# A table of half slots for the first two batches, replaced row by row, in an attention and ELU-MLP kernel

## The chip, the core and the metric

One core of one Trainium2 chip runs the whole program. The metric is the device time of one execution in microseconds (us); the figure that counts is the median of several runs. A profiled execution of the kernel before gives the trace from which all rows below are read. The engines are PE (TensorE: matmuls, with PEld for its weight loads), DVE (VectorE), ACT (ScalarE), POOL (GpSimd) and SP (SyncE, which here only issues DMAs). Each engine works through its own list of instructions in a fixed order; engines wait for each other by semaphores.

## The reference

Eight batches of twelve heads, 448 positions, head size 64. Queries and keys are normalised (RMS norm with a gain), scores are softmaxed and multiplied with the values; the result, one row of 768 per position, goes through a two-layer MLP with ELU.

```python
q_n, k_n = (rmsnorm(q, g_q), rmsnorm(k, g_k))
scores = scale * np.matmul(q_n, k_n.transpose(0, 1, 3, 2))
attn = np.exp(scores - np.max(scores, axis=-1, keepdims=True))
attn = attn / (np.sum(attn, axis=-1, keepdims=True) + 1e-09)
attn_out = np.matmul(attn, v)
h = x @ w_in                       # x: 3584 x 768, w_in: 768 x 2048
g = np.where(h > 0.0, h, np.exp(np.minimum(h, 0.0)) - 1.0)
out = g @ w_out                    # w_out: 2048 x 768
```

## The kernel before

**Tiles.** Heads are taken in pairs, 48 pairs `p`, six to a batch. The 896 query rows of a pair make seven tiles of 128, so there are 336 tiles `T` (pair `T // 7`), 42 to a batch. Each operand is split into a high and a low float16 part, and products are summed from several matmuls.

**Steps of a pair.** `load_qk` (L330) brings q and k of the pair in (448 KB, tile `nat`). `qk_square` (ACT, L353), `qk_sum` (DVE), `qk_root` (ACT, L361 and L362), `qk_newton` (DVE) and `qk_norm` (POOL) normalise; `k_high`, `q_high` (ACT, L391 and L401), `k_low`, `q_low` make the float16 parts; `qk_transpose` (SP, L420, two DMA transposes, one of q and one of k) turns them into `qkt`; `q_swap` (SP, L427, two copies of 112 KB inside the chip's memory) adds the halves in swapped order, and every score tile needs all three.

**Steps of a tile.** `s_mm` (PE, L537) makes the scores in one of the PSUM banks `s0` to `s4`; `s_max` (DVE, L544), `s_exp` (ACT, L558), `s_z`, `s_rec`. In batch 0 (T below 42) the probabilities are turned on PE: `s_diag` (POOL, L574) makes a diagonal matrix, `s_pe` (PE, L582) multiplies with it, `s_hi` (ACT, L592) copies the result out of the bank, which is then free. From T = 42 on, `s_hi` (L598) and `s_lo` (DVE, L603) write float16 parts, and `s_tr` (SP, L613) is a DMA transpose into `ptall`. `attend` (PE, L630) multiplies with v once per pair; `x_high` (ACT, L637) and `x_low` hand the result to the MLP.

**Weights.** Sixteen pieces of `w_in` and 24 of `w_out` are brought in by `conv.load` (SP, L229; 768 KB and 512 KB) and split in steps: `s_act` (L237) and `s_bits` (L240) on ACT, `s_shift` (L245), `s_join` (L269), `s_scale` and `s_low` (L290) on DVE, `s_high` on POOL, and `s_sums` (L142, column sums on PE). All of it happens while batches 0 and 1 go through attention.

**MLP.** `mlp(b)` makes 576 matmuls for batch b, first the layer of `w_in` (L730), then that of `w_out` (L741). For batch 0 it can begin in earnest only when all six pairs of batch 0 have been attended to. Afterwards these matmuls fill PE between the score tiles of the next batch.

**What sets the order.** A half slot `h` is a place in a list, not a time: for h from -18 up, the program writes down all steps due at h - 0.5 and at h, loads first, then other steps, then the matmuls of h, then the late PE steps. So h fixes the order of the instructions on each engine and nothing else; an engine that is behind simply works the list off later. The half slots stand in the table `SCHED` (from L864): `qk` (one row a pair, in the order of the steps above, from `load_qk` to `q_swap`), `v`, `scan` (loads of v, for its scale), `wi` and `wo` (one row a weight piece), `tile` (one row a tile), `mm` (half slot of each `s_mm`), `att`, `rate` (MLP matmuls due by each h), `m`, `m1`, `m2`. Rows are given for the first two batches; the last row of `qk`, `v`, `scan` and `tile` is repeated for all later pairs, batches and tiles with a fixed distance.

```python
for p in range(NP):
    k = p if p < 12 else 11
    put([h + HP * (p - k) for h in SCHED["qk"][k]], [
        (load_qk, p), (qk_square, p), (qk_sum, p), (qk_root, p), (qk_newton, p), (qk_norm, p),
...
    run_tasks(h - 0.5, 1)
    run_tasks(h - 0.5, 2)
    run_tasks(h, 0)
    run_tasks(h, 1)
```

All DMAs are issued by SP in this order, on one queue.

Of the kernel before, what the change touches and what calls it, by code (L numbers as in the profile page):

```python
# [1137 lines left out]
```

## Time and profile before

| what | value |
|---|---|
| median of 3 runs | 1234.65 us (1234.53 to 1234.99) |
| the profiled execution's own time | 1238.01 us |
| its span from first to last instruction | 1236.2 us |
| PE busy | 1185.0 us (96%) |
| DVE busy | 863.4 us (70%) |
| ACT busy | 808.2 us (65%) |
| POOL busy | 499.1 us (40%) |
| DMA moved | 181.29 MB |

The shares are means over stages that differ: in the first of 40 slices PE is busy for 3 tenths and from the tenth slice on for 9 tenths or more, while DVE and ACT stand at 8 or 9 tenths in the first nine slices and at 5 to 7 tenths later. So the table is to be read by stage.

### The profile page before, as it was taken

What the parts mean: (1) busy time and instruction counts of PE and PEld (TensorE: products, weight loads), DVE (VectorE), ACT (ScalarE), POOL (GpSimd) and SP (SyncE); (2) the same over time, 40 slices, a digit from 0 to 9 for tenths busy, and PEclk for the clock granted to TensorE, in tenths of its full rate; (3) what the DMA queues carried; (4) which work ended last, traced back from release to release, by engine and by line L of the source; (5) the groups of instructions that cost most, each with busy time, mean ns of one, the idle gap of its engine ahead of it and who ended that gap; (6) DMA issues with size and microseconds to landing.
All of it is one profiled execution on the core that took longest, in us unless ns stands there. A gap on an engine that the chain in (4) does not pass through costs nothing.

```text
span 1236.2 us, 21611 instructions
## 1 busy us (share of the span) xinstructions
PE 1185.0 (96%) x7180; PEld 736.4 (60%) x7180; DVE 863.4 (70%) x2042; ACT 808.2 (65%) x1705; POOL 499.1 (40%) x789
## 2 busy tenths in 40 slices
PE   3778899999999999999999999999999999999998
PEld 2556455765557655675557655675557655675576
DVE  7889999888885588666885588566785588542410
ACT  7889999867775477556675477556675477542310
POOL 4767554644444343444344343444344344320000
PEclk9889999999999999999999999999999999999999
DMA  8766889879667876687668867687568766551000
GB/s 302 224 155 189 190 185 188 164 175 193 134 137 165 177 137 135 138 195 153 128 131 162 184 139 131 137 199 150 130 131 165 181 137 134 109 108 31 1 16 30
DMA packets 403024, 181.29 MB, mean 147 GB/s; under 512 B 368352, under 2 KB 385376, under 8 KB 402912
## 3 DMA queue, kind: packets, MB, share of 16 engines
q1 hardware_dynamic: 402912, 179.91, 66.8%
q8 instruction: 57, 0.93, 0.3%
q14 instruction: 55, 0.45, 0.1%
HBM read 68.35 MB, written 11.01 MB: 64 GB/s over the span
## 4 chain that ended last, share of the span: by engine, by line
PE 82%; DVE 4%; issue 0%; ACT 0%; POOL 0%; ACTq 0%
PE m L741 23%; PE m L730 22%; PE s L741 12%; PE s L730 11%; PE s L537 9%; PE av L630 7%; DVE p L603 1%; DVE st L544 0%; DVE gall L687 0%; DVE w32s L269 0%; DVE e L674 0%; DVE wlos L312 0%; PE av L142 0%; DVE wts L245 0%; ACT s L558 0%
## 5 line engine op out<-in xcount | busy, mean ns | idle before, releaser
L544 DVE TENSOR_REDUCE st<-s 128x1 f32<-128x448 f32 x336 | 207.3, 620 | 168.4 <-PE s L537 166.8
L741 PE MATMUL m<-gall,whos 128*128 128x448 f16 x1024 | 282.0, 353 | 0.0
L562 POOL TENSOR_SCALAR st<-st 128x1 f32<-128x1 f32 x294 | 74.3, 253 | 482.2 <-ACT s L558 475.2
L741 PEld LDWEIGHTS <-whos 128*128 128x128 f16 x1536 | 221.7, 144 | 73.4 <-issue 0.7
L730 PE MATMUL m<-x,whi 128*128 128x448 f16 x926 | 256.4, 353 | 0.3 <-DVE e L674 0.3
L558 ACT ACTIVATE s<-s,st 128x448 f32<-128x448 f32 x294 | 178.1, 606 | 100.0 <-DVE st L544 98.6
L730 PEld LDWEIGHTS <-whi 128*128 128x128 f16 x1536 | 149.8, 98 | 137.2 <-issue 1.7
L598 ACT ACTIVATE p<-s,st 128x448 f16<-128x448 f32 x294 | 185.1, 631 | 61.2 <-DMA ptall<-p 35.9
L603 DVE SCALAR_TENSOR_TENSOR p<-s,st,p 128x448 f16<-128x448 f32 x294 | 198.6, 677 | 30.8 <-ACT p L598 29.6
L537 PE MATMUL s<-qkt 128*128 128x448 f16 (+1 forms) x768 | 184.8, 360 | 18.0 <-ACT gall L592 5.3
L741 PE MATMUL m<-gall,wlos 128*128 128x448 f16 x512 | 181.3, 354 | 0.0
L730 PE MATMUL m<-x,wli 128*128 128x448 f16 x463 | 163.3, 353 | 0.0
L741 PE MATMUL s<-gall,whos 128*128 128x448 f16 x512 | 140.8, 353 | 0.0
L741 PEld LDWEIGHTS <-wlos 128*128 128x128 f16 x768 | 110.6, 144 | 41.6 <-issue 6.8
L730 PE MATMUL s<-x,whi 128*128 128x448 f16 x450 | 124.0, 352 | 0.0
L730 PEld LDWEIGHTS <-wli 128*128 128x128 f16 x768 | 75.1, 98 | 74.2 <-issue 6.8
L537 PEld LDWEIGHTS <-qkt 128*128 128x128 f16 (+1 forms) x768 | 63.3, 101 | 79.4 <-issue 34.5
L684 ACT ACTIVATE gall<-e,ui 128x448 f16<-128x448 f32 x128 | 85.1, 665 | 32.1 <-DVE e L679 32.1
L630 PE MATMUL av<-ptall,vt 128*64 128x448 f16 x924 | 94.7, 353 | 0.6 <-DVE most L145 0.6
L687 DVE SCALAR_TENSOR_TENSOR gall<-e,ui,gall 128x448 f16<-128x448 f32 x128 | 88.0, 688 | 8.5 <-ACT gall L684 8.3
L382 POOL TENSOR_TENSOR nat<-nat,r 128x896 f32<-128x896 f32 (+1 forms) x48 | 84.4, 1758 | 21.8 <-DVE r L372 13.5
L741 PE MATMUL s<-gall,wlos 128*128 128x448 f16 x256 | 90.6, 354 | 0.0
(120 smaller groups left out, 1696.5 us busy)
## 6 DMA issues: line engine op xcount, KB each, us to landing
nat<-in_qk SPq DMA_DIRECT2D x48, 448.0 KB, 4.6
...
qkt<-qkt SPq DMA_DIRECT2D x96, 112.0 KB, 4.1
...
whos<-in_w_in SPq DMA_DIRECT2D x10, 768.0 KB, 6.6
ptall<-p SPq DMA_TRANSPOSE x336, 3.0
```

Source lines behind the costliest of these rows:

```text
L382: nc.gpsimd.tensor_tensor(out=n[:, a:], in0=n[:, a:], in1=r[:, a:], op=ALU.mult)
L537: nc.tensor.matmul(ps[r0 : r0 + n, :S], lhs, qq[:, 1, h * S : h * S + S], start=(t == 0), stop=(t == 2),)
L544: nc.vector.tensor_reduce(out=st[:, 0:1], in_=pss[T][:, :S], axis=AX.X, op=ALU.max, negate=True)
L558: nc.scalar.activation(e, ps, AF.Exp, bias=st[:, 0:1], accum_out=st[:, 1:2])
L562: (nc.vector if by_pe(T) else nc.gpsimd).tensor_scalar(out=st[:, 1:2], in0=st[:, 1:2], scalar1=1e-9, scalar2=2.0 ** (UP - 7) if by_pe(T) e ...
L598: nc.scalar.activation(p16[:, :S], pss[T][:, :S], AF.Copy, scale=stats[T][:, 2:3])
L603: nc.vector.scalar_tensor_tensor(out=p16[:, S:], in0=ps[:, :S], scalar=r, in1=p16[:, :S], op0=ALU.mult, op1=ALU.subtract)
L630: nc.tensor.matmul(av[64 * h : 64 * h + 64, :S], vs[:, h], ps[h], start=(k == 0), stop=(k == len(terms) - 1),)
L684: nc.scalar.activation(g[:, 0], e, AF.Copy, scale=ui)
L687: nc.vector.scalar_tensor_tensor(out=g[:, 1], in0=e, scalar=ui, in1=g[:, 0], op0=ALU.mult, op1=ALU.subtract)
L730: nc.tensor.matmul(ph[:, :S], w[:, c, :], x[:, r, :], start=(c == 0 and i == 0), stop=last)
L741: nc.tensor.matmul(py[:, :S], w, g[:, r, :], start=(f == 0 and i == 0), stop=last)
```

## The change

The table `SCHED` is replaced; no function, tile or transfer changes, and every step is still there once. Nearly every row of `qk`, `v`, `scan`, `wi`, `wo`, `tile`, `rate`, `m1`, `m2`, `mm` moves some entries by a half to several half slots. Two rows of each kind:

```diff
     "qk": [
-        [-18, -17, -16.5, -14.5, -13.5, -13.5, -10, -10.5, -10, -4.5, -9.5, -6.5, -3.5, -3.5],
-        [-16.5, -15.5, -10, -10, -9.5, -2.5, -1.5, -1, 1, 3, 2.5, 4, 6.5, 11.5],
...
-        [5, 8.5, 12.5, 13, 19, 19.5, 20.5, 22, 22, 34.5, 31, 32.5, 35, 35],
...
+        [-16, -16, -15.5, -15, -13, -12.5, -10, -9.5, -9.5, -8, -9, -7.5, -5, -4.5],
+        [-18, -14, -13, -8, -7.5, -4.5, -3, -3, 1, 3, 3.5, 6.5, 4.5, 11.5],
...
+        [5.5, 8.5, 11, 15.5, 15.5, 19.5, 21.5, 20, 23.5, 33.5, 28.5, 32, 35, 37.5],
...
     "tile": [
...
-        [0, 1, 2, 3, 4, 4.5, 6, 9, 5],
...
+        [0, 1, 2, 3.5, 4.5, 5, 6, 13.5, 7.5],
...
     "mm": [
-        [-1, -2, 1, -1, 5, 8, 7, 12, 16, 15, 20, 20, 21, 24, 23, 30, 29, 31, 34, 34, 38, 37, 42,
...
+        [-1, -4, 0, 1, 6, 7, 8, 12, 16, 17, 19, 20, 21, 24, 24, 29, 28, 30, 32, 36, 39, 40, 40,
```

What this does to the order of instructions is shown at three places.

**SP at the start of the program, before.** `nat_143` is pair 0, `nat_159` pair 1, `nat_239` pair 2, `qkt_216` pair 0; `in_w_in` is a weight piece, `in_v` a piece of v.

```order
L330 DMA nat_143<-in_qk 128x896
L190 DMA ggt_145<-in_gg 128x128
L330 DMA nat_159<-in_qk 128x896
L229 DMA raws_133<-in_w_in 128x1536
L172 DMA gall_131<-in_v 128x512 x2
L229 DMA raws_133<-in_w_in 128x1536
L229 DMA whos_121<-in_w_in 128x1536 x2
L420 DMA_TRANSPOSE qkt_216<-t16_194 128x7x128 x2
L427 DMA qkt_216<-qkt_216 64x896 x2
L330 DMA nat_239<-in_qk 128x896
```

The same place now, where `nat_143` is pair 1, `nat_156` pair 0, `nat_241` pair 2 and `qkt_210` pair 0:

```order
L330 DMA nat_143<-in_qk 128x896
L190 DMA ggt_145<-in_gg 128x128
L330 DMA nat_156<-in_qk 128x896
L229 DMA raws_133<-in_w_in 128x1536 x2
L172 DMA gall_131<-in_v 128x512
L229 DMA whos_121<-in_w_in 128x1536 x2
L420 DMA_TRANSPOSE qkt_210<-t16_198 128x7x128
L172 DMA gall_131<-in_v 128x512
L330 DMA nat_241<-in_qk 128x896
L420 DMA_TRANSPOSE qkt_210<-t16_198 128x7x128
L427 DMA qkt_210<-qkt_210 64x896 x2
```

Pair 0, the one that is needed first, is now loaded third instead of first, and a piece of v and pair 2 are loaded between the two transposes of pair 0, ahead of its swap.

**ACT around tiles 20 and 21, before.** `x1` is the output of pair 1; `ex_891` is `s_exp` of tile 20 (bank `s0`), `ex_923` that of tile 21 (bank `s1`, the first tile of pair 3); `raws` are weight steps, `t16` and `qkt` steps of pairs 4 and 5.

```order
L637 ACTIVATE x1_124<-av_72,vs_474 128x448
L558 ACTIVATE ex_880,st_846<-s4_71,st_846 128x448
L391 ACTIVATE t16_883<-nat_602 128x7x64
L237 ACTIVATE wts_134<-raws_133 128x768
L558 ACTIVATE ex_891,st_876<-s0_67,st_876 128x448
L592 ACTIVATE ptall_132<-s2_69 112x4x128
L353 ACTIVATE qkt_898<-nat_835 128x896
L240 ACTIVATE raws_133<-raws_133 128x768
L592 ACTIVATE ptall_132<-s3_70 112x4x128
L401 ACTIVATE t16_883<-nat_602 128x7x64
L558 ACTIVATE ex_923,st_908<-s1_68,st_908 128x448
```

The same place now, where `ex_913` is tile 20 and `ex_929` tile 21:

```order
L637 ACTIVATE x1_124<-av_72,vs_455 128x448
L558 ACTIVATE ex_850,st_837<-s4_71,st_837 128x448
L592 ACTIVATE ptall_132<-s0_67 112x4x128
L237 ACTIVATE wts_134<-raws_133 128x768
L391 ACTIVATE t16_870<-nat_599 128x7x64
L240 ACTIVATE raws_133<-raws_133 128x768
L592 ACTIVATE ptall_132<-s2_69 112x4x128
L353 ACTIVATE qkt_885<-nat_829 128x896
L401 ACTIVATE t16_870<-nat_599 128x7x64
L558 ACTIVATE ex_913,st_893<-s0_67,st_893 128x448
L558 ACTIVATE ex_929,st_911<-s1_68,st_911 128x448
```

Four steps that came after the exponential of tile 20 (the `s_hi` of bank `s2`, the square of pair 5, `s_bits`, `q_high` of pair 4) now stand ahead of it.

**PE at the same place, before.** The two matmuls of tile 21 into `s1` read `qkt_661` (pair 3); those of tile 20 into `s0` read `qkt_390` (pair 2).

```order
L582 MATMUL s1_68<-dgz_824,ex_771 112x128 x4
L582 MATMUL s0_67<-dgz_830,ex_738 112x128 x4
L537 LDWEIGHTS qkt_661
L537 MATMUL s1_68<-qkt_661 128x448
L537 LDWEIGHTS qkt_661
L537 MATMUL s1_68<-qkt_661 128x448
L537 LDWEIGHTS qkt_390
L537 MATMUL s0_67<-qkt_390 128x448
```

The same place now, with `qkt_385` for pair 2 and `qkt_670` for pair 3:

```order
L582 MATMUL s0_67<-dgz_806,ex_777 112x128 x4
L537 LDWEIGHTS qkt_385
L537 MATMUL s0_67<-qkt_385 128x448
L537 LDWEIGHTS qkt_385
L537 MATMUL s0_67<-qkt_385 128x448
L730 LDWEIGHTS wli0_105
L730 MATMUL m0_73<-x0_123,wli0_105 128x448
L582 MATMUL s2_69<-dgz_863,ex_839 112x128 x4
L537 LDWEIGHTS qkt_670
L537 MATMUL s1_68<-qkt_670 128x448
```

Tile 20 now comes before tile 21, with one MLP matmul and one `s_pe` between them.

## Rows read from the trace of the kernel before

**Rows 1.** Busy time by stage (header names the columns).
```profile
core 0: us, PE busy (x) PEld busy (x) DVE busy (x) ACT busy (x) POOL busy (x), PEclk, DMA share, GB/s
0.00:20.00 20.00, 2.15 (x27) 1.59 (x27) 13.21 (x35) 13.86 (x17) 5.95 (x10) 1.00 0.81 267
20.00:146.00 126.00, 99.80 (x814) 69.46 (x815) 113.03 (x307) 116.84 (x221) 86.34 (x95) 0.95 0.70 205
146.00:220.00 74.00, 70.65 (x488) 38.09 (x485) 71.86 (x170) 71.99 (x141) 37.75 (x55) 1.00 0.87 178
220.00:1160.00 940.00, 939.82 (x5475) 576.62 (x5474) 653.94 (x1514) 593.41 (x1310) 367.95 (x627) 1.00 0.70 144
```

**Rows 2.** Timeline of ACT, 70 to 86 us: start, us; idle before it in brackets.
```profile
75.83 0.94 ACT L237 ACTIVATE wts<-raws 128x768 f32<-128x768 f32 x1
80.67 0.63 ACT L558 ACTIVATE ex<-s,st 128x448 f32<-128x448 f32 x1 [3.91 <-PE s L582]
...
81.30 0.59 ACT L592 ACTIVATE ptall<-s 112x512 f32<-112x512 f32 x1
81.78 0.95 ACT L353 ACTIVATE qkt<-nat 128x896 f32<-128x896 f32 x1
82.62 1.92 ACT L240 ACTIVATE raws<-raws 128x768 uint16<-128x768 uint16 x1
84.28 0.69 ACT L592 ACTIVATE ptall<-s 112x512 f32<-112x512 f32 x1
84.86 0.56 ACT L401 ACTIVATE t<-nat 128x448 f16<-128x448 f32 x1
85.32 0.63 ACT L558 ACTIVATE ex<-s,st 128x448 f32<-128x448 f32 x1
```

**Rows 3.** Timeline of PE, 70.5 to 81 us.
```profile
74.35 0.35 PE L537 MATMUL s<-qkt 128*128 128x448 f16 x1 [1.34 <-DMA qkt<-t]
76.82 1.28 PE L537 MATMUL s<-qkt 128*128 128x448 f16 x3 [2.12 <-DMA qkt<-qkt]
```

**Rows 4.** Issues on SP, 60 to 80 us: start, us to issue.
```profile
67.39 0.58 SPq L229 DMA_DIRECT2D raws<-in_w_in  x1
68.70 1.23 SPq L420 DMA_TRANSPOSE qkt<-t  x1
70.03 1.18 SPq L427 DMA_DIRECT2D qkt<-qkt  x2
```

**Rows 5.** DMA issues at 67.4 and 70.6 us: KB, us from issue to landing.
```profile
raws<-in_w_in SPq DMA_DIRECT2D x1, 768.0 KB, 5.8
...
qkt<-qkt SPq DMA_DIRECT2D x1, 112.0 KB, 6.1
```

**Rows 6.** Timeline of ACT, 0 to 32 us: the first squares and the first exponential.
```profile
4.32 0.95 ACT L353 ACTIVATE ptall<-nat 128x896 f32<-128x896 f32 x1 [2.30 <-DMA nat<-in_qk]
7.55 0.95 ACT L353 ACTIVATE ptall<-nat 128x896 f32<-128x896 f32 x1 [2.29 <-DMA nat<-in_qk]
...
22.74 0.63 ACT L558 ACTIVATE ex<-s,st 128x448 f32<-128x448 f32 x1 [0.27 <-DVE st L544]
```

**Rows 7.** Timeline of PE, 0 to 45 us: the first score tile's second matmul.
```profile
20.53 2.77 PE L537 MATMUL s<-qkt 128*128 128x448 f16 x7 [1.36 <-DMA qkt<-qkt]
```

**Rows 8.** Timeline of ACT, 30 to 50 us: its waits.
```profile
33.62 0.95 ACT L353 ACTIVATE qkt<-nat 128x896 f32<-128x896 f32 x1 [0.63 <-PE s L537]
...
42.16 0.60 ACT L592 ACTIVATE ptall<-s 112x512 f32<-112x512 f32 x1 [2.32 <-PE s L582]
```

**Rows 9.** Two later pairs: SP and PE around the attention; all `ptall` landings, 460 to 1060 us.
```profile
559.56 1.25 SPq L613 DMA_TRANSPOSE ptall<-p  x1
...
566.64 2.25 PE L630 MATMUL av<-ptall,vt 128*64 128x448 f16 x22
...
589.89 2.25 PE L630 MATMUL av<-ptall,vt 128*64 128x448 f16 x22
...
DMA to landing us min/median/max: 2.5/3.0/5.5
```

More of the change, by code (lines that the diff above doesn't have):

```diff
@@ L1043 @@
-        [0, 1, 2, 3, 4, 4.5, 6, 9, 5],
+        [-0.5, 1, 2.5, 4, 5, 5, 7],
+        [-2, -0.5, 0, 1, 1.5, 4, 4.5],
+        [2, 3, 4, 4, 5, 10, 10.5],
+        [1.5, 5, 6.5, 9.5, 9.5, 11, 13],
+        [9.5, 10.5, 10.5, 11, 12.5, 12.5, 14],
+        [9, 10, 10, 11, 14.5, 17, 18],
+        [10, 13, 13, 13, 16, 16.5, 17.5],
+        [13.5, 14, 15.5, 15.5, 18, 18.5, 19],
+        [17, 19.5, 20.5, 21.5, 21.5, 22, 24],
+        [18.5, 19, 20, 20, 20, 20.5, 24],
+        [21, 22, 22.5, 23.5, 24.5, 25, 28],
@@ new lines @@
+        [20.5, 21.5, 21.5, 23, 25.5, 26, 27.5],
+        [22.5, 24.5, 26, 26, 26.5, 27, 29.5],
+        [24.5, 27, 27.5, 28, 29, 29.5, 31],
+        [25.5, 28, 29, 29.5, 29.5, 30.5, 34],
+        [31, 33, 33.5, 35, 35, 36.5, 37.5],
+        [29, 32.5, 33, 34, 34, 35, 36.5],
+        [32, 36.5, 37.5, 37.5, 38, 39, 39.5],
+        [33.5, 36, 37.5, 40, 40.5, 41.5, 42.5],
+        [36.5, 37.5, 38.5, 38.5, 40, 41.5, 42.5],
+        [40.5, 41, 42, 43, 44, 46, 46.5],
+        [41, 42, 42, 42, 44, 45.5, 47],
@@ new lines @@
+        [43, 44, 45, 45.5, 46, 47, 48.5],
+        [45, 46, 46.5, 46.5, 47, 48, 49.5],
+        [48, 50, 50, 51, 51.5, 52.5, 53.5],
+        [48.5, 48.5, 49, 51, 52.5, 53.5, 56],
+        [50, 50.5, 54, 55.5, 56, 56, 57],
+        [51.5, 56, 57, 57, 58, 58.5, 59.5],
+        [56, 57, 57.5, 57.5, 59, 59.5, 62],
+        [56, 59, 59.5, 60.5, 61, 61, 62.5],
+        [59, 60, 62, 63, 64, 65, 67.5],
+        [60, 60, 64.5, 66, 67.5, 67.5, 68.5],
+        [61.5, 63.5, 64.5, 65, 66, 69.5, 70.5],
+        [64.5, 66.5, 67, 68, 70.5, 70.5, 73],
@@ new lines @@
+        [67.5, 68.5, 69.5, 70.5, 71, 71, 73],
+        [69.5, 70.5, 71, 72, 72, 73, 75.5],
+        [73, 74.5, 75, 76, 77.5, 77.5, 80],
+        [73, 73.5, 73.5, 74.5, 74.5, 77, 77.5],
+        [75.5, 76, 78, 79, 80, 81, 82],
+        [76.5, 82, 82.5, 82.5, 84, 84, 84.5],
+        [78, 79.5, 79.5, 80.5, 80.5, 83, 86],
+        [81.5, 82.5, 83.5, 84, 85.5, 86.5, 87],
+        [82.5, 83.5, 86.5, 87.5, 88.5, 91, 93],
+        [84, 86, 86, 89.5, 90, 91.5, 95],
+        [87.5, 88, 88, 91.5, 93, 94, 99],
@@ new lines @@
+        [91, 92, 94, 94, 94, 95, 96.5],
+        [90.5, 92.5, 95, 95, 96, 98, 100],
+        [94, 95, 97, 97, 98, 100, 102],
+        [96.5, 97.5, 98.5, 99.5, 100.5, 100.5, 101],
+        [101, 101.5, 101.5, 102.5, 103.5, 105, 109],
+        [96.5, 103, 103.5, 104, 104, 105.5, 107.5],
+        [102.5, 103, 103, 105, 107, 108, 111],
+        [105.5, 107, 108.5, 109, 110, 110, 110.5],
+        [107.5, 109, 111, 111.5, 113, 113, 116],
+        [109.5, 110.5, 112, 112.5, 113, 113, 113],
+        [112, 112.5, 112.5, 113, 114, 114, 115.5],
@@ new lines @@
+        [113, 115, 115, 115, 116.5, 117.5, 124.5],
+        [115, 116, 116, 117, 117.5, 118.5, 120.5],
+        [116.5, 116.5, 118.5, 118.5, 119.5, 120, 123],
+        [119.5, 121, 121, 122, 123.5, 126, 128.5],
+        [120, 121.5, 122, 122.5, 123.5, 124.5, 127],
+        [122, 124, 126.5, 127, 127.5, 128.5, 130],
+        [125, 126, 126, 126.5, 127.5, 127.5, 130],
+        [128.5, 128.5, 129, 129.5, 131.5, 132, 141],
+        [127.5, 130, 130, 131, 131.5, 132.5, 134.5],
+        [130, 131.5, 132, 132, 132.5, 133.5, 135],
@@ new lines @@
+        [132, 133.5, 133.5, 134.5, 135.5, 137, 138],
+        [135.5, 137.5, 138.5, 140, 141.5, 142, 142],
+        [134.5, 136, 138.5, 138.5, 142, 142, 144],
+        [135, 135, 138.5, 141, 141.5, 141.5, 142],
+        [140.5, 140.5, 143.5, 144, 145, 146, 150],
+        [142.5, 143, 143, 143.5, 144, 144, 148],
+        [146.5, 147, 147, 148.5, 148.5, 149, 149],
+        [148.5, 148.5, 152.5, 154, 154, 154.5, 156.5],
+        [148, 149.5, 150, 151.5, 151.5, 152, 155],
+        [147.5, 148.5, 151.5, 154, 155, 155, 157],
@@ new lines @@
+        [152, 152.5, 153, 154, 155.5, 155.5, 157.5],
+        [156.5, 157.5, 157.5, 157.5, 159, 159.5, 162.5],
+        [158.5, 158.5, 159.5, 160.5, 161.5, 162.5, 162.5],
+        [157.5, 158.5, 160, 160, 161, 162.5, 165],
+        [158.5, 159.5, 162, 162.5, 165, 166.5, 168.5],
+        [163, 163.5, 163.5, 163.5, 163.5, 166, 168],
+        [163.5, 163.5, 165, 166, 167, 167, 169],
+        [165, 167, 167.5, 168.5, 169.5, 169.5, 169.5],
+        [169.5, 170, 171, 171.5, 173, 174, 176],
+        [168, 168.5, 171.5, 171.5, 175, 175.5, 179],
@@ L1070 @@
-        [2.5, 3.5, 3.5, 5.5, 6.5],
-        [1.5, 2.5, 3, 3.5, 4.5],
+        [0.5, 1, 2.5, 6.5, 11.5],
+        [1.5, 3, 3.5, 6, 6],
+        [2.5, 5.5, 6, 8, 9],
+        [2, 3.5, 3.5, 6, 7.5],
+        [2, 2, 3.5, 4.5, 8],
+        [0.5, 1, 2, 3, 5],
+        [1.5, 2.5, 4, 5, 12.5],
+        [1, 2.5, 3, 5, 6],
+        [2.5, 4.5, 5, 6, 6.5],
+        [1.5, 3.5, 4.5, 6, 6.5],
+        [1.5, 2, 3.5, 4.5, 10],
+        [1, 1, 2.5, 5.5, 6.5],
+        [1, 1.5, 2, 5, 8],
+        [2, 2, 3.5, 7.5, 9.5],
@@ L1074 @@
     "m2": [
[L1075 to L1080 removed]
+        [5, 7.5, 8],
+        [4.5, 12, 16],
+        [2.5, 10.5, 13],
+        [8.5, 10, 14.5],
+        [3.5, 7.5, 13],
+        [4.5, 7, 9.5],
         [1, 2, 3],
```

156 lines of the change are left out of this document (26 added, 130 removed), and 127 rows, old and new, of the table SCHED.

## The prediction

> **What bounds the kernel now.** I read the stages first [rows 1]. From 220 us on, PE is busy for 939.82 of 940 us: nothing that happens on the other engines there can be seen in the time, and the number of matmuls does not change. From 146 to 220 us PE is busy for 70.65 of 74 us, so at most 3.35 us are to be had. From 0 to 146 us PE has 101.95 us of work in 146 us. That is where the time can move. The MLP of batch 0 cannot begin before the last pair of batch 0 has been attended to, and until then PE lives on what the others hand it. Of those, ACT is the fullest: 116.84 of 126 us from 20 to 146 us, against 113.03 on DVE and 86.34 on POOL. So up to 146 us the pace is ACT's list, and a microsecond comes off the end only if ACT's idle time shrinks there or if its list becomes shorter.
>
> ACT's idle time, 9.16 us in that stage, lies for the most part in three places, which its timeline shows. At 80.67 us ACT had sat idle for 3.91 us in front of an exponential [rows 2]; at 42.16 us for 2.32 us in front of an `s_hi`, and at 33.62 us for 0.63 us [rows 8]. PE shows why for the first: its list is in order, and at 74.35 and 76.82 us it stood, for 1.34 and 2.12 us, in front of the first tile of pair 3 until a transpose and then a swap of that pair had landed [rows 3], while tile 20, which ACT wanted, was ready behind it. And SP shows why the swap was late: a weight piece of 768 KB was issued at 67.39 us, ahead of the transpose at 68.70 and the swaps at 70.03 [rows 4]. It took 5.8 us to land, and a swap of only 112 KB took 6.1 us [rows 5]. Transfers land one behind the other, and a small one pays for the large one ahead of it.
>
> **Part 1: tile 20 goes ahead of tile 21.** On PE the tile that needs the swap of pair 3 now comes after tile 20 and an `s_pe`, and on ACT four steps come ahead of the exponential of tile 20 that used to follow it. Counted from start to start of the next row, these are 0.48 us (`s_hi`, 81.30 to 81.78), 0.84 us (square, to 82.62), 1.66 us (`s_bits`, to 84.28) and 0.46 us (`q_high`, 84.86 to 85.32) [rows 2], together 3.44 us. So even if PE served tile 20 as late as now, ACT would idle for only 3.91 - 3.44 = 0.47 us; if PE serves it earlier, the whole 3.91 us go. The swap itself is not sooner: the same weight piece still stands ahead of the second transpose of pair 3, and now the load of pair 5 stands ahead of the swap too. What is late next is therefore the exponential of tile 21, which follows directly; it stood at 85.32 us, 8.6 us after the last swap landed (70.6 + 6.1 = 76.7), so there is room. I take -3.7 us (-3.9 to 0).
>
> **Part 2: the start.** Pair 0 is loaded third. The two loads of equal size were followed by squares at 4.32 and 7.55 us, each of which had waited for its load [rows 6], so the first data that anything can be done with come 3.23 us later. In front of the first exponential (22.74 us) ACT has the same steps in both lists. Lower bound: ACT idled for 2.29 us ahead of 7.55 us anyway, and only the first square, 0.95 us, is pushed behind it: +1.0 us. Upper bound: the whole 3.23 us, and on top a wait for the two loads that now go between the transposes of pair 0. The first tile already waited 1.36 us for its swap at 20.53 us [rows 7], and a load of half the size of a weight piece ahead of a swap costs about half of what separates 6.1 us from the 2.5 us that a transfer takes at the least [rows 5, 9], so up to +1.8 us, together +5.0 us. I take +3.0 us, close to the 3.23 us that are a row: ACT's list gives less, but the scores need the late pair.
>
> The Trainium skill, "DMA: Bandwidth & Descriptors", Specifications, gives 435 GB/s as the ceiling of the fabric. By it, 448 KB and the 64 KB of gains ahead would delay pair 0 by about 1.2 us, an estimate, and with 1.2 in place of 3.0 us the sum below would come to -4.7 us; the rows say 3.23 us, and I go by them.
>
> **Part 3: what the late start absorbs.** The `s_hi` at 42.16 us waited on PE, which stood in front of pair 1's first tile until its swap had landed. Around that swap SP's list is the same: transpose, load of pair 3, transpose, one weight piece, swap. If those transfers land when they do now, an ACT that is 3 us later finds them done, and the 0.63 and 2.32 us of waiting [rows 8] are eaten: -3.0 us. If the transposes, whose input comes from ACT and POOL, are as late as everything else, nothing is eaten: 0. I take -2.9 us, since ACT's list reaches this tile more than twenty steps after the first exponential, whereas pair 1's float16 parts come early in it. Against this, the new order brings two tight places behind the first exponentials: the square of pair 2 is followed by its `qk_root` with one exponential in between, so the sum on DVE has only 0.63 us of cover, and the fifth weight piece's `s_act` comes ahead of that square. I put these at +0.7 us (0 to 2).
>
> **Part 4: the rest.** Up to the last `s_hi` of batch 0, ACT has one `s_bits` less and one exponential more ahead of it; an `s_bits` takes up to 1.92 us and an exponential 0.63 us with its read of the sum behind it [rows 2]. For a smaller `w_out` piece the difference is smaller; I take 0 (-1.1 to 0). From 146 to 220 us all engines stay full in both orders, and I see no reason for a change either way: 0 (-1.5 to +1.5).
>
> From batch 2 on, the repeated rows move too. The transpose of the last tile of each pair goes from 5 to 7.5 half slots after its tile. Today the last transpose ahead of an attention is issued at 559.56 us and the attention begins at 566.64 us, 7.08 us later; a landing takes 3.0 us in the median [rows 9], so 4.08 us are spare. A half slot does not hold SP up, though: between the old and the new place its list has nothing that waits for PE, so the issue stays where its data let it be. 0 us.
>
> **Sum.** -3.7 + 3.0 - 2.9 + 0.7 + 0 + 0 = -2.9 us. The profiled execution would go from a span of 1236.2 us to 1233.3 us and from 1238.01 us to 1235.1 us; the median stood 3.36 us below the profiled execution, so 1234.65 - 2.9 = 1231.75, say 1231.8 us.
>
> **The rivals.**
>
> *The delay is rigid (slower).* Everything in front of pair 1 hangs on pair 0: its transposes, too, slide by 3 us, so the waits at 33.62 and 42.16 us stay, and the swap of pair 3, now behind one more load, stalls the exponential of tile 21 by as much as that of tile 20 today. Then +3.0 + 0.7 with nothing gained: 1234.65 + 3.7 = 1238.4 us. For it: the in-order queue of transfers. Against it: the 3.44 us of ACT work that now covers tile 20 do not depend on pair 3. It decides if tile 21's exponential begins after about 88 us.
>
> *The late load costs little.* If ACT's list alone sets the start (+1.0 instead of +3.0 us), the sum is -4.9 us: 1229.8 us. If ACT's waits in part 3 vanish as well and PE's 3.35 us from 146 to 220 us shrink by half, it is 1228 us. The ceiling that the Trainium skill states ("DMA: Bandwidth & Descriptors", Specifications) would point this way.
>
> *One wait is exchanged for another.* The stall of tile 20 goes, but the new order loses as much between 86 and 146 us, where ACT hardly waits now (9.16 us idle in the whole stage, of which 3.91, 2.32 and 0.63 us are the waits above [rows 2, 8]): about 1234.6 us. The change would then not do what it says.
>
> *Every later pair pays.* Should the later transposes of part 4 really be issued 2.5 half slots later, the 4.08 us of slack would be used up, since one pair takes 589.89 - 566.64 = 23.25 us for 14 half slots [rows 9], so 2.5 of them are 4.15 us. Every tenth of a microsecond beyond it costs 36 pairs 3.6 us. At 0.25 us a pair: 1244 us. Nothing in SP's list speaks for it.
>
> **How the numbers follow.** About 0.2%, 2.5 us, is what a measurement of this kernel can tell from no change, so faster means below 1232.2 us and slower above 1237.1 us. My forecast (1230 to 1233.5 us) has 0.45, rather less than two thirds of it on the faster side; the cheap start 0.20, all faster; the exchange 0.15, all same; the rigid delay 0.16, mostly slower; the later pairs 0.04, slower. Faster 0.28 + 0.20 = 0.48; same 0.17 + 0.15 = 0.32; slower 0.20. Leaving out the best part of the cheap start and the later pairs, the range is 1227.0 to 1238.5 us.
>
> **What would show it right or wrong.** In the profile after: the first square at about 7.5 us and the first exponential at 25 to 26 us (part 2); the wait in front of an `s_hi` near 42 us gone (part 3); the wait near 80 us below 0.5 us and no DMA named by PE there (part 1); the last attention of batch 0 some 3 us earlier than now; PE without idle time from 220 us on (part 4). A first exponential at 23.5 us would show the cheap start, a stall in front of the first tile of pair 3 or a last attention of batch 0 that comes no earlier than now, the rigid delay.

## The result and the profile after

The changed kernel is **slower**: 1244.1 us in the median (1242.55 to 1245.0) against 1234.78 us; the ratio, as estimated from the runs, is 1.0067 (the two medians alone give 1.0075), with a 95% interval of 1.0054 to 1.0081, so 6.7 to 10 us. The forecast was 1231.8 us and a range that ended at 1238.5 us. The profiled execution took 1245.0 us, with a span of 1243.2 us.

Busy time by stage of the kernel after (same columns as [rows 1]):

```profile
0.00:20.00 20.00, 0.85 (x13) 0.84 (x14) 11.18 (x31) 12.43 (x15) 4.35 (x10) 1.00 0.70 241
20.00:146.00 126.00, 98.05 (x807) 68.68 (x808) 111.43 (x298) 115.29 (x216) 81.29 (x92) 0.93 0.71 203
146.00:220.00 74.00, 67.84 (x468) 35.52 (x465) 69.58 (x167) 71.85 (x141) 39.70 (x56) 1.00 0.89 182
220.00:1160.00 940.00, 939.22 (x5479) 576.78 (x5477) 664.78 (x1524) 599.02 (x1313) 380.24 (x629) 1.00 0.70 145
```

Beside [rows 1], PE is idle for 1.3 us more in the first stage (20 - 0.85 against 20 - 2.15), 1.75 us more in the second, 2.8 us more in the third and 0.6 us more in the last. So the loss lies ahead of 220 us, two fifths of it (2.8 of the 7.0 us between the spans of the two profiled executions) from 146 to 220 us, where I had put a zero.

ACT's timeline after, at the start and in front of tiles 20 and 21 (to be read against [rows 6] and [rows 2]):

```profile
7.58 0.95 ACT L353 ACTIVATE ptall<-nat 128x896 f32<-128x896 f32 x1 [5.56 <-DMA nat<-in_qk]
...
14.21 0.62 ACT L391 ACTIVATE t<-nat 128x448 f16<-128x448 f32 x1
...
25.88 0.63 ACT L558 ACTIVATE ex<-s,st 128x448 f32<-128x448 f32 x1 [0.59 <-DVE st L544]
...
85.61 0.62 ACT L558 ACTIVATE ex<-s,st 128x448 f32<-128x448 f32 x1
...
86.36 0.63 ACT L558 ACTIVATE ex<-s,st 128x448 f32<-128x448 f32 x1
```

Several of my signs are there: the first square at 7.58 us, the first exponential 3.1 us late, and the exponentials of tiles 20 and 21 without a wait. And still tile 20's comes 4.9 us later than in the trace of before, and the last attention of batch 0, which I had put 3 us earlier, comes later: its `x_high` begins at 149.59 us, against 145.16 us. New waits stand ahead of tile 20, which the trace of before does not have:

```profile
45.55 0.63 ACT L558 ACTIVATE ex<-s,st 128x448 f32<-128x448 f32 x1 [0.93 <-DVE st L544]
53.14 0.63 ACT L558 ACTIVATE ex<-s,st 128x448 f32<-128x448 f32 x1 [0.71 <-DVE st L544]
...
68.48 0.60 ACT L592 ACTIVATE gall<-s 112x512 f32<-112x512 f32 x1 [1.60 <-PE s L582]
```

### The profile page after: what moved, and what is told of

It is laid out like the page before. It is cut to its first block, busy times and chain, and to the rows that moved or that the text cites. A ratio compares the mean times of both kernels' runs of the same rounds, so it can differ in the third digit from the quotient of the medians.

```text
span 1243.2 us, 21624 instructions
## 1 busy us (share of the span) xinstructions
PE 1185.5 (95%) x7180; PEld 736.0 (59%) x7180; DVE 871.9 (70%) x2042; ACT 813.2 (65%) x1705; POOL 506.6 (41%) x789
## 4 chain that ended last, share of the span: by engine, by line
PE 79%; DVE 2%; ACT 2%; issue 0%; DMA 0%; ACTq 0%
PE m L741 22%; PE m L730 21%; PE s L741 11%; PE s L730 10%; PE s L537 8%; PE av L630 7%; DVE p L603 0%; DVE st L544 0%; DVE wlos L312 0%; ACT raws L240 0%; ACT p L598 0%; DMA raws<-in_w_out 0%; ACT s L558 0%; DVE w32s L269 0%; DVE e L674 0%
## 5 line engine op out<-in xcount | busy, mean ns | idle before, releaser
L544 DVE TENSOR_REDUCE st<-s 128x1 f32<-128x448 f32 x336 | 205.4, 615 | 124.7 <-PE s L537 123.9
L562 POOL TENSOR_SCALAR st<-st 128x1 f32<-128x1 f32 x294 | 86.4, 294 | 464.1 <-ACT s L558 451.9
L687 DVE SCALAR_TENSOR_TENSOR gall<-e,ui,gall 128x448 f16<-128x448 f32 x128 | 94.7, 741 | 9.1 <-ACT gall L684 9.1
L382 POOL TENSOR_TENSOR nat<-nat,r 128x896 f32<-128x896 f32 (+1 forms) x48 | 81.5, 1698 | 31.2 <-DVE r L372 25.1
```

Of the source, the lines that this page charges most:

```text
L382: nc.gpsimd.tensor_tensor(out=n[:, a:], in0=n[:, a:], in1=r[:, a:], op=ALU.mult)
L544: nc.vector.tensor_reduce(out=st[:, 0:1], in_=pss[T][:, :S], axis=AX.X, op=ALU.max, negate=True)
L562: (nc.vector if by_pe(T) else nc.gpsimd).tensor_scalar(out=st[:, 1:2], in0=st[:, 1:2], scalar1=1e-9, scalar2=2.0 ** (UP - 7) if by_pe(T) e ...
L687: nc.vector.scalar_tensor_tensor(out=g[:, 1], in0=e, scalar=ui, in1=g[:, 0], op0=ALU.mult, op1=ALU.subtract)
```

## Experiments

Times are given as ratios to the kernel before on the same chip, with 95% intervals; 0.0010 is 1.2 us. Before itself spread from 1232.5 to 1241.0 us over these comparisons.

### Another execution of the kernel before

Run `again` is the kernel before, unchanged.

> The kernel before, unchanged, profiled once more. Its profiled execution stood 3.36 us above its median. If that excess lay in the waits for the swaps of pairs 1 and 3, as two runs with the same order up to 130 us suggest (1.0 to 1.4 us and 2.6 to 2.8 us there, against 2.32 and 3.91 us), an execution near 1235 us shows about 1.2 us near 41 us and 2.7 us near 77.5 us, and its attention of pair 5 begins some 2 us earlier than at 141.8 us. If the excess lies elsewhere, those two waits are 2.3 and 3.9 us again.

It took 1235.24 us with a span of 1233.4 us, 2.8 us less than the execution that I had read. Its waits near 42 and 80 us on ACT:

```profile
42.30 0.60 ACT L592 ACTIVATE ptall<-s 112x512 f32<-112x512 f32 x1 [2.37 <-PE s L582]
...
77.18 0.63 ACT L558 ACTIVATE ex<-s,st 128x448 f32<-128x448 f32 x1 [1.25 <-PE s L582]
```

The first is as long as in [rows 8], the second is 1.25 us where [rows 2] show 3.91 us. So half of the expectation falls, and the other half is stronger than expected. Two runs further down, `last_rows` and then `late_new`, have the order of before up to this place and beyond it, and are thus two more executions of it here:

```profile
41.26 0.60 ACT L592 ACTIVATE ptall<-s 112x512 f32<-112x512 f32 x1 [1.04 <-PE s L582]
...
77.51 0.64 ACT L558 ACTIVATE ex<-s,st 128x448 f32<-128x448 f32 x1 [2.57 <-PE s L582]
```

```profile
41.09 0.60 ACT L592 ACTIVATE ptall<-s 112x512 f32<-112x512 f32 x1 [1.36 <-PE s L582]
...
77.52 0.64 ACT L558 ACTIVATE ex<-s,st 128x448 f32<-128x448 f32 x1 [2.77 <-PE s L582]
```

In these three executions the two waits differ one by one, but together they make 3.6, 3.6 and 4.1 us, and the exponential of tile 20 begins at 77.2 to 77.5 us. In the execution read ahead of the prediction they make 6.2 us, and it begins at 80.67 us.

Why the second wait differs, PE's timeline and the granted clock show. First the execution read ahead of the prediction (stage rows, then PE):

```profile
70.00:76.00 6.00, 3.36 (x34) 2.27 (x30) 4.14 (x10) 6.00 (x11) 4.68 (x5) 1.00 1.08 249
76.00:82.00 6.00, 5.18 (x30) 3.96 (x31) 3.79 (x10) 2.09 (x5) 1.91 (x3) 0.51 0.20 74
```

```profile
78.61 2.03 PE L582 MATMUL s<-dgz,ex 128*112 128x128 f32 x8
```

Then the other execution of the same kernel:

```profile
76.00:82.00 6.00, 4.18 (x37) 3.24 (x34) 6.00 (x12) 4.82 (x8) 3.62 (x4) 1.00 0.01 4
```

```profile
75.08 0.73 PE L537 MATMUL s<-qkt 128*128 128x448 f16 x3 [2.10 <-DMA qkt<-qkt]
...
76.04 1.10 PE L582 MATMUL s<-dgz,ex 128*112 128x128 f32 x8
```

In both, PE stood for more than 2 us in front of the swap of pair 3. In the first, which had stood 1.34 us in front of the transpose before that [rows 3], the granted clock then fell to half (0.51, the lower of its two levels, 1.2 and 2.4 GHz), and the eight matmuls for which the exponential waited took 2.03 us; in the second, where the stop in front of the transpose was 0.44 us, it stayed full and they took 1.10 us. Of the 2.66 us by which the two waits differ, 0.90 us are the longer stop in front of the transpose, and the rest lies behind the swap, where PE was slower. The 3.91 us were thus a transfer that was late and an engine at half speed, and the second part is not in every execution: in `last_rows` and `late_new` the granted clock from 76 to 82 us was 0.86 and 0.74.

### What makes the start late

`start_new` and `start_old` mix the two tables by the mean of the old and the new half slot (`OTHER` is the other table; `start_new` starts from the kernel before, `start_old` from the changed one):

```diff
+def take(old, new, f):
+    return [n if f((o + n) / 2) else o for o, n in zip(old, new, strict=True)]
...
+part(lambda h: h < 24)
```

> The table of before with the entries of the changed table wherever the mean of old and new half slot lies below 24 (up to about 45 us); everything behind is as before. It asks whether a late start is carried through or absorbed. Theory A, a delay of the start is rigid: the start costs what the trace after shows up to tile 20, some 4.5 us, and most of it comes out at the end: 1237 to 1240 us, and the first exponential at 25 to 26 us. Theory B, the delay is absorbed by the waits of ACT near 42 and 80 us, and what was lost was lost behind: 1234 to 1236 us.

> The counterpart: the changed table with the entries of before wherever the mean half slot lies below 24. Theory A, rigid start: the 4.5 us come back, 1238.5 to 1241 us, and about as much as the loss between 86 and 224 us (4 to 6 us) less the gain at tile 20 (3.9 us) remains. Theory B, the loss is all behind the start: 1243 to 1244 us. If start and rest simply add, the differences of this run and of the run with the new start alone add up to that of the whole change.

`start_new`: 1.0061 (1.0047 to 1.0075). `start_old`: 1.0045 (1.0031 to 1.0058); in it the shift of one weight piece stands ahead of the `s_act` whose result it should shift, so its columns of the hidden layer are garbage, and the amount of work is the same. Neither theory holds: both halves lose. Nor do they simply add: 0.0061 and 0.0045 make 0.0106, more than the whole change. The traces say the same. `x_high` of pair 5, the last of batch 0, begins at 141.69 us in `again` and at 149.59 us in the kernel after, 7.9 us later; in `start_new` and then in `start_old` it is 5.2 and 5.0 us late:

```profile
146.88 0.62 ACT L637 ACTIVATE x<-av,vs 128x448 f16<-128x448 f32 x1
```

```profile
146.67 0.63 ACT L637 ACTIVATE x<-av,vs 128x448 f16<-128x448 f32 x1
```

What the new start costs in the changed kernel is the difference between that kernel and `start_old`: 2.9 us at this place, and 1.0067 - 1.0045 = 0.0022, 2.7 us, in the time. (Of the repeated rows, `start_new` took over only that of the tiles.)

`loads_old`, `start_loads`, `start_pieces` and `start_between` take the start apart. The first is the changed kernel with one edit, the others are the kernel before with one edit each:

```diff
+SCHED["qk"][0][0], SCHED["qk"][1][0] = -18, -16
```
```diff
+SCHED["qk"][0][:3], SCHED["qk"][1][0] = [-16, -16, -15.5], -18
```
```diff
+SCHED["wi"][:2] = [
+    [-15, -14, -12, -13, -8.5, -12.5, -7, -4.5, -2.5],
+    [-15, -12.5, -9.5, -7, -7, -7, -6, 0.5, 7.5],
+]
```
```diff
+SCHED["qk"][2][0], SCHED["scan"][0][1] = -5, -6
```

> The changed table with nothing but the first loads of pair 0 and pair 1 put back in the old order (half slots -18 and -16). If the 3.1 us by which the first exponential came later are due to the order of these two loads alone and are carried to the end: first exponential back at 22 to 23 us and 1240.5 to 1241.5 us. If the rest of the new start makes up for it or loses it anyway (a transpose and a swap behind a load of pair 2): 1243 to 1244 us.

> The kernel before with only the first loads exchanged: pair 1 first, pair 0 third, the square of pair 0 where its data let it be. The prediction counted 3.0 us for this (3.23 us of lateness carried through): first exponential at 25.7 us. The rival 'the late load costs little': k_high of pair 0 stands behind the first weight piece's s_act and s_bits on ACT anyway (12.01 us), so it moves by 1 us or less and the first exponential stays below 24 us; time 1235 to 1236 us.

> The kernel before with only the rows of the first two weight pieces from the changed table: the second piece is loaded earlier, and ACT reads it ahead of the first k_high. In the run loads_old the first exponential stayed 3.3 us late although pair 0 was loaded first again, and ACT stood in front of these pieces until they had landed (9.69 and 11.60 us). If that is what makes the start late: k_high of pair 0 at about 14 us in place of 12.0, the first exponential 2 us later, and 1236 to 1238 us. If the loads between the transposes of pair 0 make the start late: first exponential at 22.7 us as before and no change.

> The kernel before with only two loads moved: the load of pair 2 and one piece of v go between the two transposes of pair 0, ahead of its swap. If these make the start late: the second transpose lands 2 to 4 us later (18.6 us before), and the first exponential comes at 24.5 to 26 us. If the transposes get through all the same: first exponential near 22.7 us. Time in both cases 1234.5 to 1237 us, since the waits near 42 us and 77 us take up a part.

`loads_old`: 1.0065 (1.0051 to 1.0080), nothing gained. Its ACT timeline:

```profile
9.69 0.89 ACT L237 ACTIVATE wts<-raws 128x768 f32<-128x768 f32 x1 [0.91 <-DMA raws<-in_w_in]
11.60 0.90 ACT L237 ACTIVATE wts<-raws 128x768 f32<-128x768 f32 x1 [1.02 <-DMA raws<-in_w_in]
...
14.04 0.62 ACT L391 ACTIVATE t<-nat 128x448 f16<-128x448 f32 x1
```

Pair 0 is there early, but ACT now stands in front of two weight pieces that come ahead of `k_high` (L391), and that step begins at 14.04 us, against 14.21 us in the kernel after. The load order, on which my 3.0 us rested, is hidden behind the pieces. By itself it costs little: in `start_loads` the first exponential begins at 23.72 us, 0.98 us later than in [rows 6], and the time is 1.0003 (0.9994 to 1.0013). `start_pieces` alone does more (1.0010, 0.9999 to 1.0020):

```profile
11.21 0.92 ACT L237 ACTIVATE wts<-raws 128x768 f32<-128x768 f32 x1 [1.01 <-DMA raws<-in_w_in]
...
13.66 0.62 ACT L391 ACTIVATE t<-nat 128x448 f16<-128x448 f32 x1
...
25.40 0.63 ACT L558 ACTIVATE ex<-s,st 128x448 f32<-128x448 f32 x1
...
49.06 0.66 ACT L558 ACTIVATE ex<-s,st 128x448 f32<-128x448 f32 x1
```

The first exponential is 2.66 us late; the last line is that of tile 8. In `start_between` (1.0004, 0.9994 to 1.0015) it begins at 24.11 us, 1.37 us late, and ACT waits 2.37 us for a transpose:

```profile
21.05 0.58 ACT L391 ACTIVATE t<-nat 128x448 f16<-128x448 f32 x1 [2.37 <-DMA qkt<-t]
...
24.11 0.63 ACT L558 ACTIVATE ex<-s,st 128x448 f32<-128x448 f32 x1
```

So three edits, one by one, delay the start by 1.0, 2.7 and 1.4 us, and the changed kernel, which has them all, by 3.1 us: the longest one covers most of the others, and undoing one that is covered (`loads_old`) gives nothing. No run undoes the pieces alone.

### Pair 1: is it the order of its transposes?

The rows of SP's order around the swap of pair 1 read alike in both kernels, but in the changed one k is transposed ahead of q. The swap copies q, and SP waits for it:

```profile
SPq L427 <- DMA qkt<-t: 2.9, 1, 2.9
```

(SP's waits of the kernel after, 25 to 45 us: total, times, longest; in another execution of before that row reads 0.5 us.) `after_q_first` puts q first again in the changed kernel, `before_k_first` puts k first in the kernel before, and `after_repaired` adds to the former the old loads, the old first two weight pieces and one step on DVE:

```diff
+SCHED["qk"][1][9:13] = [3.5, 3, 4.5, 6.5]
```
```diff
+SCHED["qk"][1][9:13] = [2.5, 3, 6.5, 4]
```
```diff
+SCHED["qk"][1][9:13] = [3.5, 3, 4.5, 6.5]
+SCHED["qk"][0][0], SCHED["qk"][1][0] = -18, -16
+SCHED["wi"][:2] = [
+    [-15, -13.5, -11.5, -11.5, -8.5, -11, -3.5, -1.5, -1],
+    [-11.5, -10, -7, -7, -7, -6.5, -2, -1.5, 6.5],
+]
+SCHED["tile"][46][5] = 97
```

> The changed kernel with q again ahead of k in pair 1: q_low ahead of k_low, and the transpose of q ahead of that of k. In the changed table k comes first, so that the swap, which copies q, stands 2.9 us on SP until the second transpose has landed behind the load of pair 3. If that is why the waits near 42 us absorb nothing: the swap is issued near 35.5 us in place of 38.4, tile 8's exponential comes 2 us or more earlier, and the time is 1241.5 to 1243 us. If the late start alone carries through: swap and tile 8 as before, 1244 us.

> The mirror image: the kernel before with k ahead of q in pair 1, and nothing else. If the order of the two transposes costs what after_q_first should give back: the swap of pair 1 is issued near 34.5 us in place of 32.3, ACT's wait near 42 us grows by about 2 us, and the time is 1 to 2 us above that of before. If it is indifferent: no difference.

> The changed kernel with four repairs: q ahead of k in pair 1, the first two loads and the rows of the first two weight pieces as in before, and the s_lo of tile 46 one half slot earlier, ahead of the sum of squares of pair 9. If the start's pieces and the transposes are what is late in the first 60 us: first exponential near 23.5 us in place of 25.9, tile 8 some 4 us earlier than in the changed kernel. If that lateness is carried to the end: 1239 to 1241 us; if the order behind gives it back: above 1242 us. PE's stall near 161 us goes from 1.9 to about 1 us if the place of s_lo on DVE is its cause.

The swap did come earlier, issued at 35.78 us against 38.36 us in the kernel after:

```profile
35.78 1.13 SPq L427 DMA_DIRECT2D qkt<-qkt  x2
```

But the exponential of tile 8 did not (52.1 us, against 51.7 us in the kernel after), and the time is 1.0077 (1.0065 to 1.0089). `before_k_first`: 1.0005 (0.9996 to 1.0013). The theory falls: the order of the transposes costs SP 2.9 us and the kernel nothing. `after_repaired` gains nothing either, 1.0085 (1.0073 to 1.0098): its first exponential comes at 23.70 us, but that of tile 0 at 26.60 us, still as late as in the kernel after (26.88 us). Its DVE timeline shows why: between the maxima of the two tiles (L544) stands 2.2 us of work on weight pieces, the old rows of the pieces among the new rows of the tiles:

```profile
23.05 0.62 DVE L544 TENSOR_REDUCE st<-s 128x1 f32<-128x448 f32 x1 [2.02 <-PE s L537]
...
24.37 1.66 DVE L290 SCALAR_TENSOR_TENSOR wli<-w32s,ws,whi 128x768 f16<-128x768 f32 x1
25.95 0.61 DVE L544 TENSOR_REDUCE st<-s 128x1 f32<-128x448 f32 x1
```

So this run does not tell what the repaired start alone is worth. And its repair on DVE only moves a stall of PE: in the kernel after PE stands 1.91 us at 161.16 us and 0.78 us at 170.96 us, in this run 0.92 us at 159.22 us, as expected, and 1.71 us at 169.95 us.

### Pair 3, and a faster version

`pair3_new` and `pair3_only` put the changed entries of half slots 24 to 56 into the kernel before, `tile20_first` only the exchange of tiles 20 and 21 on PE, `swap1_first` only one weight load behind the swap of pair 1, and `swaps_first` the same for pairs 1 and 3:

```diff
+part(lambda h: 24 <= h < 56)
```
```diff
+SCHED["mm"][0][20:22] = [37, 38]
```
```diff
+SCHED["wi"][8][0] = 12
```
```diff
+SCHED["wi"][8][0] = 12
+SCHED["wi"][12][:3] = [36, 40.5, 41]
```

> The table of before with the entries of the changed table wherever the mean half slot lies from 24 up to below 56 (about 45 to 105 us): tile 20 goes ahead of tile 21, the start and all from pair 5 on stay. If the 3.9 us won at tile 20 are kept up to the end: 1231 to 1232 us. If the new order of this stretch gives them back behind it, or the stages behind take them up: 1234 to 1236 us. If it loses more than it wins: above 1236 us.

> The table of before with the changed entries from half slot 24 up to below 56 alone, each tile and each weight piece taken whole. Unlike the run pair3_new, in which one weight piece was joined before its shift, so that its columns of the hidden layer were garbage, all of the computation is there. If the 2 us that the stretch wins up to the attention of pair 5 are kept: 1232 to 1233.5 us. If the stages behind take them up: 1234 to 1236 us.

> The kernel before with two entries changed: PE makes the scores of tile 20 ahead of those of tile 21. It measures what the wait at 80 us (3.91 us in the first profile, 2.6 to 2.8 us in others) is worth at the end. If a microsecond of ACT's idle time in batch 0 is a microsecond of the whole: the wait is gone and 1231.5 to 1232.5 us. If other waits grow in its place: 1234 to 1235 us.

> The kernel before with one entry changed: the weight piece of 768 KB that SP issues just ahead of the swap of pair 1 is issued just behind it. If a small transfer pays for the large one ahead of it, the swap lands near 36 us in place of 39.5 us, ACT's wait near 41 us (1.0 to 2.3 us) goes, and the time is 1232.5 to 1234 us. If the swap is late for another reason (its transposes), it lands as before and nothing changes: 1234.5 to 1235.5 us.

> The kernel before with the weight piece ahead of the swap of pair 1 put behind it (the run swap1_first, 0.9983 of before), and the same for pair 3, whose piece's steps on ACT move behind q_high of pair 4. If the swap of pair 3 pays for the piece ahead of it: it lands 2 to 3 us sooner, PE's idle time at 72 to 77 us shrinks from over 4 us to 2 us or less, its clock stays at full speed, and the time is 0.5 to 1.5 us below swap1_first: 0.997 to 0.998 of before. If the late piece is then what ACT waits for: no better than swap1_first.

`pair3_new` (1.0010, 1.0000 to 1.0020; the columns of one weight piece garbage as in `start_old`) has no wait in front of tile 20, but two new ones ahead of it:

```profile
55.33 0.89 ACT L237 ACTIVATE wts<-whos 128x768 f32<-128x768 f32 x1 [1.91 <-PE m L142]
...
64.02 0.60 ACT L592 ACTIVATE gall<-s 112x512 f32<-112x512 f32 x1 [1.17 <-PE s L582]
```

One wait is exchanged for another, not behind 86 us, as my rival had it, but ahead of the tile. `pair3_only` (1.0041, 1.0028 to 1.0054) settles nothing: in this mix the scores of tiles 16 and 17 go into the banks of tiles 11 and 12 before those are copied out, so PE lacks two waits, and its loss has causes of its own. In `tile20_first` the scores of tile 20 likewise go into the bank of tile 15 before that is copied out. Its time is 0.9999 (0.9987 to 1.0011): in its profile tile 20 waits 0.99 us and, at 87.17 us, an `s_hi` 1.21 us. Not every wait here is the edit's: `last_rows`, with the order of before at this place, has one of 1.20 us at 88.88 us in front of an `s_hi` too, and in both runs the granted clock from 82 to 88 us was 0.72, against 1.00 in `again`. The stall that I priced at 3.7 us is worth nothing that can be measured, and by the interval no more than 1.6 us.

`swap1_first` is **faster than both kernels**: 0.9983 (0.9973 to 0.9994), about 2 us. The median landing of the swap's two halves, for another execution of before and then for this run (DMA issues, 27 to 40 us: KB, us):

```profile
qkt<-qkt SPq DMA_DIRECT2D x2, 112.0 KB, 6.7
```

```profile
qkt<-qkt SPq DMA_DIRECT2D x2, 112.0 KB, 3.3
```

The wait near 42 us is gone from its ACT timeline, and the exponential of tile 20 begins at 75.14 us, 2.0 us earlier than in `again`. So a small transfer does pay for the large one ahead of it. `swaps_first`, 1.0008 (0.9998 to 1.0018), gives the gain back: PE's wait for the swap of pair 3 shrinks to 0.73 us, and behind it PE waits for a diagonal of POOL, with the clock at half again afterwards (0.51 from 82 to 88 us):

```profile
82.82 2.05 PE L582 MATMUL s<-dgz,ex 128*112 128x128 f32 x8 [4.16 <-POOL dgz L574]
```

### The later stages and the repeated rows

`late_new` is the changed table behind half slot 84 on the old one, `early_new` the old one behind 80 on the changed one; tiles and weight pieces are taken whole. `last_rows` is the kernel before with the repeated rows of the changed table:

```diff
+part(lambda h: h < 84)
```
```diff
+part(lambda h: h < 80)
```
```diff
+for key in ("qk", "v", "scan", "tile"):
+    SCHED[key][-1] = OTHER[key][-1]
```

> The table of before up to half slot 84 (start, batch 0's tiles, all that ACT does up to about 135 us) and the changed table behind it, repeated rows included. It asks whether the 3.2 us that the changed kernel loses between the attentions of pairs 5 and 11 come with the order of batch 1 itself or are a consequence of reaching it late. Theory A, the order of batch 1 costs them by itself (an s_lo that frees a bank stands too far down DVE's list, and the matmul behind it waits 1.9 us near 160 us): 1238 to 1239 us, PE idle from 146 to 220 us about 6 us. Theory B, the loss is only what arrives late from batch 0: 1235 to 1236 us, PE idle about 3.5 us.

> The counterpart: the changed table up to half slot 80, that of before behind it, its repeated rows too. Theory A (batch 1's order costs 3.2 us by itself): what is left is the start and batch 0, +2 to +4 us on before, 1237 to 1239 us, PE idle from 146 to 220 us 3.5 to 4 us. Theory B: nearly the whole loss stays, 1241 us or more.

> The table of before with only the repeated rows (the last of the rows of pairs, v, scan and tile) from the changed table. The run start_new had them too, and there PE stood still for 1.0 us at 339 us until a transpose of probabilities had landed, so that its time mixes the start with these rows. If the later transposes of the last tile of each pair cost nothing, as the trace after says (PE idle 0.8 us from 220 to 1160 us): 1234 to 1236 us. If every later pair pays a little: 1237 us or more, and PE waits for ptall in front of attentions.

`late_new`: 1.0069 (1.0055 to 1.0083), `early_new`: 1.0096 (1.0081 to 1.0111), each as bad as the whole change or worse. Both have a stall of PE close behind the place where the tables meet, 2.25 us at 147.22 us and 2.96 us at 149.28 us, longer than any that the kernels before and after have from 140 to 160 us. So they suggest that rows of the two tables do not fit each other, and do not price batch 1. `last_rows`: 1.0037 (1.0024 to 1.0050). Here, too, the loss is at the place where they meet, the first tiles on repeated rows:

```profile
312.56 0.57 PE L537 MATMUL s<-qkt 128*64 128x448 f16 x4 [2.42 <-DVE p L603]
```

Before and behind that stretch its attentions follow each other as in the kernel before, and in the kernel after PE stands only 0.78 us in all from 220 to 1160 us. Later pairs pay nothing.

## Where the time went, and why the prediction was wrong

The stretches between the same instructions tell it best: the exponentials of tiles 0, 8, 16, 22 and 38 on ACT, and `x_high` of pairs 5 and 7. First the other execution of the kernel before (run `again`), cut there:

```profile
0.00:23.40 23.40, 4.88 (x36) 2.68 (x36) 16.66 (x40) 16.86 (x20) 9.13 (x12) 1.00 0.82 272
23.40:48.00 24.60, 17.22 (x144) 13.45 (x144) 22.69 (x61) 21.25 (x42) 17.60 (x18) 0.93 0.78 248
48.00:65.50 17.50, 13.71 (x134) 9.97 (x131) 16.46 (x45) 17.47 (x35) 12.43 (x14) 1.00 0.80 263
65.50:82.90 17.40, 12.87 (x101) 7.79 (x100) 14.29 (x35) 16.14 (x28) 12.78 (x13) 1.00 0.54 145
82.90:124.00 41.10, 35.92 (x313) 24.60 (x313) 38.70 (x112) 40.33 (x81) 26.88 (x32) 1.00 0.68 189
124.00:141.70 17.70, 13.70 (x118) 9.10 (x118) 16.82 (x52) 17.52 (x38) 12.62 (x17) 1.00 0.74 201
141.70:197.40 55.70, 51.72 (x355) 28.14 (x355) 54.08 (x131) 53.63 (x107) 28.35 (x41) 1.00 0.95 194
```

The same for the kernel after:

```profile
0.00:26.90 26.90, 4.48 (x40) 2.73 (x41) 16.63 (x41) 16.56 (x21) 8.97 (x12) 1.00 0.79 261
26.90:51.70 24.80, 17.58 (x143) 12.41 (x142) 22.68 (x64) 22.00 (x41) 17.83 (x18) 0.86 0.86 234
51.70:69.00 17.30, 13.59 (x105) 10.09 (x102) 14.45 (x39) 14.58 (x30) 11.30 (x13) 0.90 0.61 209
69.00:88.70 19.70, 15.19 (x136) 10.52 (x135) 16.84 (x43) 19.66 (x33) 13.41 (x16) 0.91 0.57 170
88.70:129.20 40.50, 34.78 (x305) 24.11 (x303) 37.70 (x102) 38.88 (x78) 25.26 (x31) 1.00 0.68 183
129.20:149.60 20.40, 16.45 (x127) 10.87 (x126) 17.76 (x59) 19.62 (x39) 10.33 (x15) 0.92 0.73 199
149.60:207.00 57.40, 52.15 (x363) 27.80 (x363) 54.04 (x129) 55.32 (x108) 31.98 (x46) 1.00 0.92 184
```

The differences of the lengths are +3.5, +0.2, -0.2, +2.3, -0.6, +2.7 and +1.7 us, together 9.6 us. ACT's busy time (the fourth pair) grows by 3.4 us in all, from 183.2 to 186.6 us, its idle time by 6.2 us, of which 3.8 us lie in the first stretch (10.34 against 6.54 us) and 2.7 us in the third (2.72 against 0.03 us). Some of ACT's work also moved across the cuts: the third stretch has 2.9 us less of it and the fourth 3.5 us more, the fifth 1.5 us less and the sixth 2.1 us more, so these are best read in pairs. The granted clock was lower than in `again` in four of the seven (0.86 against 0.93 in the second, 0.90, 0.91 and 0.92 against 1.00 in the third, fourth and sixth); what that costs no run tells apart.

In the terms of my sum, where I had -3.7, +3.0, -2.2 (that is -2.9 + 0.7) and 0 us, the stretches read +2.1 us from tile 8 to tile 22, +3.5 us up to tile 0, +0.2 us from tile 0 to tile 8, and +3.8 us behind tile 22.

**What bounds the kernel** was right: the time is made ahead of 220 us, and ACT's list sets the pace there.

**Part 1, -3.7 us: the wait went, its price was wrong.** The wait is gone. But I took its 3.91 us from one execution that stood 3.36 us above the median, and its excess over the other execution, 3.91 - 1.25 = 2.66 us, is nearly all of the 2.8 us between their spans. Three other executions with this order have 2.1 to 2.6 us less in the two waits near 42 and 80 us together and reach the exponential of tile 20 3.1 to 3.5 us earlier, so a large part of that price was this execution's own, and the change could not take it out of the median. They still wait there, 1.25 us where they had waited 2.37 us near 42 us, and 2.57 and 2.77 us where they had waited 1.04 and 1.36 us; so the two waits, which I counted as separate gains in parts 1 and 3, do not look independent. In the changed kernel ACT waits ahead of it instead, 2.72 us from tile 8 to tile 16 (at 53 and 68 us above all), and from tile 8 to tile 22 it takes 37.0 us, against 34.9 us in `again`. The trace had warned me: [rows 3] show two stops of PE, the stage row above the clock at 0.51 behind them, and the releaser in [rows 2] is PE, not a DMA. The Trainium skill, "TensorE: Matmul & The Clock Gate", HAM oscillation, says that a wait for a DMA between two bursts of matmuls can leave the engine at half clock, so that the wait costs more than its length. The runs here agree (2.03 against 1.10 us for the same eight matmuls), and add that it does not happen in every execution.

**Part 2, +3.0 us: size right, cause wrong.** The first exponential came 3.1 us late, and beside `start_old` 2.7 us of that arrived at the end. That the size came out was luck: the load order, on which it rested, accounts for 1.0 us, my own lower bound and the rival "the late load costs little". I had noted that ACT has the same steps ahead of the first exponential in both lists, and did not ask which of them come ahead of `k_high`: there, the second weight piece does it.

**Part 3, -2.9 + 0.7 us: wrong.** From tile 0 to tile 8 the changed kernel takes 24.8 us, against 24.6 us: nothing was absorbed. In the old order a late start is absorbed in part: in `start_pieces` it is 2.6 us late at tile 0 and 1.1 us at tile 8, both beside `again`. In the new order the wait at 42 us is gone, but waits at 36.35 and 45.55 us (0.75 and 0.93 us) and 0.75 us more of ACT's work stand in its place. "SP's list is the same around that swap" was false as well, since two rows that read alike were q and k exchanged; the runs show that this was harmless. `start_new`, which has the old rows behind half slot 24, does not catch up either (beside `again` 2.7 us late at tile 0, 3.0 us at tile 8), so the cause lies in the rows ahead of that half slot. Which of them it is, is not settled.

**Part 4, zero: the largest error.** With the start of before, the changed table still loses 0.0045, 5.5 us. The places, in the kernel after beside `again`, are tiles 8 to 22 (+2.1 us, 1.5 us of it more waiting on ACT), tile 22 to the end of batch 0 (+2.1 us, 1.5 us of it more waiting) and the first two pairs of batch 1 (+1.7 us, in which ACT is busy 1.7 us longer); `start_old` alone is longer than `again` in the same three, by 3.2, 2.1 and 2.1 us. So the zero was wrong in both of its halves, up to the last `s_hi` of batch 0 and from 146 to 220 us. I had compared the kinds and numbers of steps ahead of a landmark, which are nearly equal, and taken "all engines stay full in both orders" for "no change". No run prices these stretches one by one, since mixed tables stall where they meet; that part of the cause stays open. The zero for the later pairs was right.

**The rivals.** "The delay is rigid" came true in part 2 and 3, though not at the place by which I would have known it (the exponential of tile 21 begins at 86.36 us, not after 88 us); "one wait is exchanged for another" came true in part 1, ahead of the tile and not behind it; and both at once were not among the cases. The range ended 5.6 us short of the time.
